# Spectral mixing after a short convolution on one core: who issues the output stores, and which buffer the half tiles use

## The chip, the core and the metric

The kernel runs on one core of one Trainium2 chip. The time is the device time of one execution in microseconds; a time given without more is the median of five runs. A profile is one more execution, recorded by the hardware profiler, and it has its own time and its own span (first to last instruction).

The engines are PE (TensorE), DVE (VectorE), ACT (ScalarE), POOL (GpSimd) and SP (SyncE). Data between memory and the core's buffers goes through 16 DMA engines. SP and POOL issue the transfers here: the profile calls SP's queue "hardware_dynamic" (q1) and POOL's "software_dynamic" (q0).

## What is computed

The input x has 8 batches of 3264 rows and 192 columns, in float32. First a causal convolution of seven taps runs down the rows, with one softmax-normalised set of taps for each of eight groups of 24 columns. Then the rows are transformed (`rfft`), the lowest 64 modes are multiplied by complex 192 x 192 matrices, one per mode, and transformed back; the result is added to its input and passed through a 192 x 192 matrix with a rectifier:

```python
X = np.fft.rfft(x, axis=1)                      # x: result of the convolution
Y[:, :64] = einsum('bmd,mde->bme', X[:, :64], w_r + 1j * w_i)
u = x + np.fft.irfft(Y, n=S, axis=1)
out = u + np.maximum(u @ w_ch, 0)               # 8 x 3264 x 192, float32
```

(The second line is shortened: the reference does it in real and imaginary parts.)

## The kernel before

**Stages.** The rows of a batch are cut into 25 full tiles of 128 rows and a half tile of 64. Batches go in four pairs (q = 0 to 3). Until about 53 us POOL issues the loads of x (L149), converted to bfloat16 on the way; PE convolves them with banded matrices held in the tile `band` (L305), and ACT and DVE copy the result into `xall`, where it stays. PE also computes the 64 modes as matmuls with cosine and sine tables. Until about 107 us the mode matrices are loaded by POOL (L426) into `arena` and `cc`, and PE applies them. `band` is read by the convolution alone. `arena` is free of the mode matrices when the last stage begins.

**The last stage, from about 108 us.** The list `duos` holds 55 items in the order in which they are worked. There are 52 items of work on tiles and three numbers among them (items 2, 8 and 11), which stand for the preparation of the next pair's coefficients. The tile items are:

- four items of two neighbouring tiles of one pair (items 0, 1, 3, 4), each stored with two transfers of 192 KB at L578;
- 45 items of one tile of two pairs, that is of four batches (items 5 to 52, but for the numbers and the half tiles), each stored with one transfer of 384 KB at L573;
- item 14, the half tiles of all eight batches (`("h",)`), stored with four transfers of 96 KB at L554, each from 64 partitions;
- the last two, items 53 and 54, of one tile of one pair, stored with one transfer of 192 KB each at L563.

For each item PE multiplies the transposed convolution result by the channel matrix (`c_part`, L494, twelve matmuls) and adds the first part of the inverse transform (`m_part(n, 0)`, L514, or L506 for the half tiles). ACT rectifies in place (`relu`, L540). PE adds the second part (`m_part(n, 1)`), and `finish` lets DVE add `xall` into an output buffer (L565; L546 for the half tiles; L560 for the single tiles) and issues the store. The order is written out by hand in the loop at the end: for each n, `m_part` and `relu` of item n, `c_part` of item n + 1, then the second `m_part` and `finish` of item n - 1. Four PSUM tiles (`za`, `zb`, two of each) take turns.

**Output buffers.** Six buffers of 3 KB per partition lie in `arena`:

```python
NO = 6
outs = [arena[:, OB * i:OB * (i + 1)]... for i in range(NO)]
...
o = outs[n % NO]
```

A buffer is written again by the item whose number is six higher (a number in the list leaves its turn out). DVE waits until the store from it has landed. The half tiles (item 14) use buffer 2, which item 20 uses next.

**Who issues.** SP issues all stores but the four of the half tiles, which POOL issues. POOL's last transfer before those is a load at L225, at 99 us. SP's only earlier transfer is the load of the taps. Each of SP's and POOL's queues works in order, and an issue waits for the DVE addition that it stores.

Of the kernel before, what the change touches and what calls it, by code (L numbers as in the profile page):

```python
# [12 lines left out]
F32 = mybir.dt.float32  # L13
# [6 lines left out]
def kernel(  # L20
# [9 lines left out]
    nc = tc.nc  # L30
# [22 lines left out]
    def sb(name, shape, dtype, **kw):  # L53
        return pool.tile([P] + shape, dtype, tag=name, name=name, **kw)
# [23 lines left out]
    band = sb("band", [H, 2 * P], BF16)  # L78
# [18 lines left out]
    NO = 6  # L97
    OB = 2 * 2 * 2 * D
    outs = [arena[:, OB * i:OB * (i + 1)].bitcast(F32).rearrange("p (k d) -> p k d", k=2) for i in range(NO)]
    assert NO * OB <= NW * WGB  # L100
    pos = [0]

    def temp(n, dtype):
# [36 lines left out]
    def slot(q, t):  # L140
        return NT * q + t
# [48 lines left out]
    for g in range(4):  # L190
        dst, srcv = band[32 * g:32 * g + 32, :, 32 * g:32 * g + PW], pk3[32 * g:32 * g + 32, :, :]
# [213 lines left out]
    for k, u in enumerate(units):  # L405
# [5 lines left out]
        if k:  # L411
            q, t0, n = units[k - 1]
# [117 lines left out]
    duos = [((q, t), (q, t + 1)) for q in range(2) for t in (0, 2)]  # L530
# [3 lines left out]
    for k, item in ((2, 1), (8, 2), (11, 3), (14, ("h",))):  # L534
        duos.insert(k, item)

    def relu(n):
        duo, zt = items[n]
        w = D * len(duo) if duo[0] != "h" else 2 * D
        nc.scalar.activation(out=zt[:, :, 0:w], in_=zt[:, :, 0:w], func=ACT.Relu)  # L540

    def finish(n):
        duo, zt = items[n]
        o = outs[n % NO]
        if duo[0] == "h":
            nc.vector.tensor_tensor(out=o[:, :, :].rearrange("p k (a d) -> p k a d", a=2),  # L546
                                    in0=zt[:, :, 0:2 * D].rearrange("p k (a d) -> p k a d", a=2),
                                    in1=xall[:, NF:NF + NT * (NQ - 1) + 1:NT, 0, :].rearrange(
                                        "p (k a) d -> p k a d", k=2), op=ALU.add)
            for k in range(2):  # L550
                for h, r in enumerate(ROWS):
                    dst = bass.AP(tensor=out.tensor, offset=out.offset + ((4 * k + (h ^ k)) * S + P * NF) * D,
                                  ap=[[D, HALF], [2 * S * D, 2], [1, D]])
                    nc.gpsimd.dma_start(out=dst, in_=o[r, k, :].rearrange("p (a d) -> p a d", a=2))  # L554
            return
        (q0, t0), (q1, t1) = duo[0], duo[-1]
        s = [slot(*u) for u in duo]
        ov = o[:, :, :].rearrange("p k (i d) -> p (k i) d", i=2)
        if len(duo) == 1:
            nc.vector.tensor_tensor(out=ov[:, 0:2, :], in0=zt[:, :, 0:D], in1=xall[:, s[0], :, :], op=ALU.add)  # L560
            dst = bass.AP(tensor=out.tensor, offset=out.offset + (2 * q0 * S + P * t0) * D,
                          ap=[[D, P], [S * D, 2], [1, D]])
            nc.sync.dma_start(out=dst, in_=ov[:, 0:2, :])  # L563
            return
        nc.vector.tensor_tensor(out=o[:, :, :].rearrange("p k (i d) -> p i k d", i=2),  # L565
                                in0=zt[:, :, 0:2 * D].rearrange("p i (k d) -> p i k d", k=2),
                                in1=xall[:, s[0]:s[1] + 1:s[1] - s[0], :, :].rearrange("p k i d -> p i k d"),
                                op=ALU.add)
        if t0 == t1:

            dst = bass.AP(tensor=out.tensor, offset=out.offset + (2 * q0 * S + P * t0) * D,
                          ap=[[D, P], [S * D, 4], [1, D]])
            nc.sync.dma_start(out=dst, in_=ov)  # L573
        else:
            for i in range(2):
                dst = bass.AP(tensor=out.tensor, offset=out.offset + ((2 * q0 + i) * S + P * t0) * D,
                              ap=[[D, P], [P * D, 2], [1, D]])
                nc.sync.dma_start(out=dst, in_=ov[:, i:4:2, :])  # L578

    N = len(duos)  # L580
# [42 lines left out]
    for n in range(N + 1):  # L623
        if is_duo(n) and duos[n] != ("h",):
            m_part(n, 0)
            relu(n)
        if n + 1 < N and n > 0:
            if is_duo(n + 1):
                c_part(n + 1)
                if duos[n + 1] == ("h",):  # L630

                    m_part(n + 1, 0)
                    relu(n + 1)
            else:
                q, zt = items[n + 1]
                for c in range(2):
                    zw_part(q, c, zt[:, c, :])
                for act, w in enumerate(QUARTERS):
                    zw_copy(zw[:, q, :, w, :], zt[:, :, 0:2 * D].rearrange("p c (b e) -> p c b e", b=4)[:, :, w, :],
                            act)  # L640
        if is_duo(n - 1):
            m_part(n - 1, 1)
            finish(n - 1)
# [30 lines left out]
```

## Time and profile before

| | |
|---|---|
| median of five runs | 179.85 us (179.24 to 180.22) |
| the profiled execution: time | 180.22 us |
| the profiled execution: span | 178.4 us |
| PE, DVE, ACT, POOL busy | 147.1, 113.4, 98.3, 68.3 us |
| granted PE clock, mean | 0.985 |
| memory read, written | 39.40 MB, 20.05 MB |
| stores issued by SP, 384 KB | 45, landing 4.6 us after the issue (median) |
| stores issued by SP, 192 KB | 10, landing after 2.9 us |
| stores issued by POOL, 96 KB | 4, landing after 3.2 us |
| POOL's queue q0 | 36224 packets, 20.08 MB |
| SP's queue q1 | 26624 packets, 19.69 MB |

Busy time is the time in which an engine executes; a DMA issue counts as busy on POOL and not on SP. "Landing" is the time from the start of the issue until the transfer's semaphore is complete, so that it holds the issue, the time in the queues, the data and the completion. A chain of waits is followed back from the last instruction; it ends with the last instruction of an engine and does not show what a store takes after that.

### The profile page before, as it was taken

The numbers are of one execution on the slowest core, as the hardware profiler recorded it, in microseconds if no ns is written. First come the engines' busy times: TensorE is split into PE (matmuls) and PEld (weight loads), VectorE is DVE, ScalarE is ACT, GpSimd is POOL, SyncE is SP. The second block draws the span as 40 slices with busy tenths as digits, with TensorE's granted clock in tenths as the row PEclk, the third lists the DMA queues.
The fourth block names the chain that finished last, engine by engine and source line by source line (L and its number), as shares of the span: only waits on it lengthen the run. The fifth ranks groups of instructions, "written<-read, shape, count | busy, mean of one in ns | idle before, by whom it ended". The sixth has DMA issues, their size and how long they took to land.

```text
span 178.4 us, 6302 instructions
## 1 busy us (share of the span) xinstructions
PE 147.1 (82%) x2736; PEld 108.4 (61%) x2736; DVE 113.4 (64%) x161; ACT 98.3 (55%) x135; POOL 68.3 (38%) x113
## 2 busy tenths in 40 slices
PE   0046789999999998797767679999999999999940
PEld 0033456666666665575555566966777888888820
DVE  1879564765866584344435262695787888888870
ACT  8165755544554636154354455767566777666630
POOL 7999979868865644424336100000140000000000
PEclk9999999999999999789999999999999999999997
DMA  3999999999999999999999970569789999999994
GB/s 43 169 176 188 190 190 189 192 192 194 188 191 192 204 206 207 206 207 207 206 206 206 206 116 4 174 220 329 256 218 365 366 336 365 362 352 353 299 371 166
DMA packets 62875, 40.17 MB, mean 225 GB/s; under 512 B 28800, under 2 KB 62784, under 8 KB 62848
## 3 DMA queue, kind: packets, MB, share of 16 engines
q0 software_dynamic: 36224, 20.08, 81.0%
q1 hardware_dynamic: 26624, 19.69, 32.9%
q8 instruction: 21, 0.34, 0.8%
q14 instruction: 6, 0.05, 0.1%
HBM read 39.40 MB, written 20.05 MB: 333 GB/s over the span
## 4 chain that ended last, share of the span: by engine, by line
DMA 45%; PE 30%; POOL 15%; issue 4%; DVE 3%; POOLq 0%; DVEq 0%
DMA arena<-in_moe_w_i_dram 18%; DMA xall<-in_x_dram 18%; POOL xall L149 10%; PE za L514 8%; PE zb L514 7%; PE za L494 7%; DMA cc<-in_moe_w_i_dram 7%; PE zb L494 5%; DMA out_dram<-arena 2%; DVE arena L565 2%; POOL arena L426 1%; POOL xall L219 1%; POOL out_dram L554 1%; PE zb L521 1%; DVE arena L560 1%
## 5 line engine op out<-in xcount | busy, mean ns | idle before, releaser
L149 POOL DMA_DIRECT2D xall<-in_x_dram x48 | 38.4, 808 | 6.9 <-DMA xall<-in_x_dram 4.5
L305 PE MATMUL z<-xall,band 64*64 64x192 bf16 (+3 forms) x816 | 27.6, 264 | 14.7 <-ACT band L193 10.7
L325 DVE CAST xall<-z 128x768 bf16<-128x768 f32 (+1 forms) x24 | 24.5, 1021 | 14.0 <-PE z L305 12.3
L305 PEld LDWEIGHTS <-band 64*64 64x64 bf16 x816 | 18.4, 110 | 23.2 <-ACT band L193 11.0
L323 ACT CAST xall<-z 128x768 bf16<-128x768 f32 (+1 forms) x24 | 20.4, 850 | 20.7 <-PE z L305 20.6
L494 PEld LDWEIGHTS <-cc 64*128 64x128 bf16 x600 | 27.2, 94 | 6.3 <-issue 1.4
L565 DVE TENSOR_TENSOR arena<-za,xall 128x768 f32<-128x768 f32 x26 | 24.6, 956 | 5.6 <-ACT zb L540 1.7
L540 ACT ACTIVATE za<-za 128x768 f32<-128x768 f32 (+1 forms) x27 | 21.0, 783 | 8.8 <-PE za L514 8.6
L565 DVE TENSOR_TENSOR arena<-zb,xall 128x768 f32<-128x768 f32 x23 | 21.9, 957 | 4.7 <-ACT za L540 1.8
L540 ACT ACTIVATE zb<-zb 128x768 f32<-128x768 f32 (+1 forms) x25 | 19.6, 782 | 9.0 <-PE zb L514 8.7
L331 PE MATMUL low<-xall,ftab 128*128 128x384 bf16 x100 | 22.0, 348 | 0.0
L385 PEld LDWEIGHTS <-xall 128*128 128x128 bf16 x300 | 18.5, 104 | 3.2 <-issue 0.3
L360 DVE COPY cc<-r 128x1024 bf16<-128x1024 bf16 (+1 forms) x16 | 10.2, 671 | 13.4 <-ACT xs L450 6.2
L514 PE MATMUL za<-mixa,ftab 64*128 64x384 bf16 (+1 forms) x120 | 18.2, 304 | 0.0
L514 PE MATMUL za<-mixa,fsin 64*128 64x384 bf16 (+1 forms) x120 | 18.1, 304 | 0.0
L494 PE MATMUL za<-wc,cc 64*128 64x192 bf16 x318 | 18.0, 243 | 0.1
L514 PE MATMUL zb<-mixa,ftab 64*128 64x384 bf16 (+1 forms) x100 | 16.1, 313 | 0.4 <-ACT zb L540 0.4
L514 PE MATMUL zb<-mixa,fsin 64*128 64x384 bf16 (+1 forms) x100 | 16.1, 313 | 0.0
L494 PE MATMUL zb<-wc,cc 64*128 64x192 bf16 x282 | 15.9, 243 | 0.0
L514 PEld LDWEIGHTS <-ftab 64*128 64x128 bf16 x220 | 11.9, 94 | 4.2 <-issue 2.0
L358 ACT COPY cc<-r 128x1024 bf16<-128x1024 bf16 (+1 forms) x9 | 8.9, 990 | 10.2 <-PE r L385 8.0
L554 POOL DMA_DIRECT2D out_dram<-arena x4 | 2.4, 617 | 29.5 <-DVE arena L546 29.5
(109 smaller groups left out, 184.0 us busy)
## 6 DMA issues: line engine op xcount, KB each, us to landing
out_dram<-arena SPq DMA_DIRECT2D x45, 384.0 KB, 4.6
xall<-in_x_dram POOLq DMA_DIRECT2D x24, 192.0 KB, 7.5
xall<-in_x_dram POOLq DMA_DIRECT2D x16, 240.0 KB, 7.1
arena<-in_moe_w_r_dram POOLq DMA_DIRECT2D x12, 288.0 KB, 9.2
arena<-in_moe_w_i_dram POOLq DMA_DIRECT2D x12, 288.0 KB, 10.2
out_dram<-arena SPq DMA_DIRECT2D x10, 192.0 KB, 2.9
xall<-in_x_dram POOLq DMA_DIRECT2D x8, 144.0 KB, 6.7
cc<-in_moe_w_r_dram POOLq DMA_DIRECT2D x4, 288.0 KB, 11.7
```

The costliest lines, as they stand in the source:

```text
L149: nc.gpsimd.dma_start(out=xall[:, s0:s0 + nf, i, :], in_=src)
L305: mm = nc.tensor.matmul(ov[c], band[r, h, c.start + shift + 64 * (r is UP and c is LO): c.start + shift + 64 * (r is UP and c is LO) + 64] ...
L323: nc.scalar.copy(out=dst, in_=srcv)
L325: nc.vector.tensor_copy(out=dst, in_=srcv)
L331: nc.tensor.matmul(xp, ftab[:, t, :], xall[:, slot(q, t), :, :], start=(t == 0), stop=False, skip_group_check=True)
L358: nc.scalar.copy(out=out, in_=in_)
L360: nc.vector.tensor_copy(out=out, in_=in_)
L385: nc.tensor.transpose(tp[:, P * k:P * k + P], src, ident[:])
L494: nc.tensor.matmul(zt[:, i, D * k:D * k + D], cc[r, q, 3 * t + j, :], wc[r, j, :], start=(k == 0 and j == 0), stop=False, skip_group_check ...
L514: nc.tensor.matmul(zt[:, i, D * k:D * (k + w)], tabs[c][r, t, :], zw[r, q:q + w, c, QUARTERS[which], :], start=False, stop=end and k + w = ...
L540: nc.scalar.activation(out=zt[:, :, 0:w], in_=zt[:, :, 0:w], func=ACT.Relu)
L565: nc.vector.tensor_tensor(out=o[:, :, :].rearrange("p k (i d) -> p i k d", i=2), in0=zt[:, :, 0:2 * D].rearrange("p i (k d) -> p i k d", k=2),
```

## The change

The stores of the 45 four-batch items and of the first of the two single tiles (item 53) are issued by POOL. The four stores of the half tiles are issued by SP, and so is the last single tile, as before. The half tiles get a seventh buffer in the bytes of `band`. The other items take the six old buffers in turn, without the half tiles and the three numbers being counted: items 0, 1, 3, 4, 5, 6 have the buffers 0 to 5, item 13 has buffer 4, and item 20 has buffer 4 again.

```diff
+    outs.append(band[:, :, :].rearrange("p h c -> p (h c)")[:, 0:OB].bitcast(F32).rearrange("p (k d) -> p k d", k=2))
...
+    buffers = []
+    for duo in duos:
+        buffers.append(NO if duo == ("h",) else sum(b < NO for b in buffers if b is not None) % NO
+                       if isinstance(duo, tuple) else None)
...
-        o = outs[n % NO]
+        o = outs[buffers[n]]
...
-                    nc.gpsimd.dma_start(out=dst, in_=o[r, k, :].rearrange("p (a d) -> p a d", a=2))
+                    nc.sync.dma_start(out=dst, in_=o[r, k, :].rearrange("p (a d) -> p a d", a=2))
...
-            nc.sync.dma_start(out=dst, in_=ov[:, 0:2, :])
+            (nc.gpsimd if n < N - 1 else nc.sync).dma_start(out=dst, in_=ov[:, 0:2, :])
...
-            nc.sync.dma_start(out=dst, in_=ov)
+            nc.gpsimd.dma_start(out=dst, in_=ov)
```

## The prediction

> **What bounds the kernel now.** I read the page first, then the chain of waits near the end, the windows of the last 66 us, the waits of DVE and SP, and the rows of the store lines. From 112 us on the kernel only produces output items and stores them. The windows (stretch, its length, then busy us of PE, PEld, DVE, ACT, POOL, the granted clock, DMA share, GB/s):
>
> ```profile
> 145.00:155.00 10.00, 10.00 (x181) 8.35 (x178) 8.50 (x9) 6.99 (x9) 0.00 (x0) 1.00 1.05 351
> 155.00:165.00 10.00, 10.00 (x180) 8.35 (x178) 8.32 (x10) 6.85 (x10) 0.00 (x0) 1.00 1.05 354
> ```
>
> PE never pauses and POOL is idle. The clock is full. The start of each item's L494 group in the timeline gives the pace, and the one break in it:
>
> ```profile
> 133.33 0.66 PE L494 MATMUL zb<-wc,cc 64*128 64x192 bf16 x12
> ...
> 134.47 0.66 PE L494 MATMUL zb<-wc,cc 64*128 64x192 bf16 x12
> ...
> 134.82 1.82 DVE L565 TENSOR_TENSOR arena<-za,xall 128x768 f32<-128x768 f32 x2 [0.60 <-DMA out_dram<-arena]
> ...
> 135.84 0.67 PE L494 MATMUL za<-wc,cc 64*128 64x192 bf16 x12
> ```
>
> The pace is 1.145 us an item (134.47 - 133.33). Item 20 has to wait 0.60 us for buffer 2, which the half tiles (item 14) still hold. PE's next group should start at 135.62 and starts at 135.84, so the break costs PE 0.22 us, once. The chain of waits then ends on DVE:
>
> ```profile
> 170.84 0.42 DVE arena L565
> 171.26 0.46 issue
> 171.72 0.55 DVE arena L560
> 172.26 0.00 issue
> 172.27 0.05 DVEq L560
> 172.32 0.04 issue
> 172.36 0.56 DVE arena L560
> ```
>
> The last addition ends at 172.92 but the span at 178.44: 5.5 us are store. The store lines' own rows say why (duration ns min/median/max; landing in us after the issue):
>
> ```profile
> L573 SPq DMA_DIRECT2D out_dram<-arena x45: 372/372/1219, 118.9 to 171.8; - x45
> DMA to landing us min/median/max: 2.5/4.6/5.2
> ```
>
> ```profile
> L563 SPq DMA_DIRECT2D out_dram<-arena x2: 533/668/803, 172.3 to 172.9; - x2
> DMA to landing us min/median/max: 4.6/4.7/4.7
> ```
>
> A 384 KB store can land in 2.5 us; the usual one takes 4.6. The last single tile (192 KB) takes 4.6 too, while the first 192 KB stores at L578 landed in 2.0. So it stands 2.6 us behind earlier stores. In the trace's landing events most of the 16 DMA engines finish a store of 158 to 165 us after 2.35 to 2.5 us, but four or five finish up to 2.4 us later. An engine falls behind where an instruction fetch (16 KB, 0.94 us on one engine, at 137.7, 144.0, 151.7, 159.5 and 165.4 us) sits in it, and it regains only 0.085 us per item. That regain is the pace less the drain: 384 KB at the 371 to 373 GB/s that full slices show is 1.06 us, against 1.145. The burst of five stores after 168.8 us then adds about 1 us on all engines. The profiled execution took 180.22 us (span 178.44 and 1.78 around it), 0.37 above the median of 179.85. I take the difference from the span and carry it to the median.
>
> **The half tiles.** They leave the ring of six buffers and get a seventh (band, last read by the convolution), so item 20 waits for item 13's buffer, long landed. Gain 0.22 us, and nothing waits for the seventh buffer. Their four stores move from POOL (four issues of 0.61 us) to SP (0.37 to 0.5 us each), behind SP's last L578 store of 118.3 us. SP then has nothing but the last tile, 44 us later. Cost nothing; were SP held up, only this buffer would be late.
>
> **45 + 1 stores from SP to POOL.** SP's issue is 0.37 us for a store. On POOL the nearest row is L149 (738/772/1035 ns). The loads of it with the same 512 rows take 0.74 to 0.79, so 0.76. POOL wakes later: L546 ends at 128.42 and POOL starts at 128.71 (0.29 us), SP 0.03 us after its addition. One store thus takes at most 0.29 + 0.76 = 1.05 us of POOL, under the pace of 1.145. POOL is otherwise idle since 99.3 us, so behind each waiting store only the next one queues.
>
> From the start of a POOL issue to its first packet are 1.22 us (128.71 to 129.93), from SP's 0.91. A POOL store with empty DMA engines so lands about 0.29 + 1.22 + 0.14 (issue 0.76 for 0.62) + 0.95 to 1.06 of data + 0.37 = 3.0 us after its addition, against 2.5 now. A buffer is wanted again after 6 x 1.145 - 0.96 = 5.9 us, so 2.9 us of cover remain, and the added 0.5 is hidden. Without that cover it would cost up to 0.5 us per round of six items.
>
> **The drain.** This decides. In the trace's packet records SP's stores go in packets of 768 bytes, 36 ns each. The POOL stores of L554 go in packets of 4,608 and 1,536 bytes, six and two rows each; the shortest take 178 and 65 ns. 178 ns for 4,608 bytes on 16 engines is 414 GB/s, or 0.95 us for a 384 KB store. Most of L554's packets took longer (median 295 ns, about 230 to 250 GB/s), but there only 64 partitions are read, and 178 is seen where no second packet ran. So the bounds are 0.95 and 1.7 us per store, with SP's 1.06 between. I take 0.95, since the full-width stores read all partitions. It regains 0.19 us an item instead of 0.085, and over the 30 items after 136 us that is 5.7 us per engine, more than the largest lag seen (2.4 us).
>
> The Trainium skill (DMA: Bandwidth & Descriptors, "Issuing engines are not separate DMA queues") speaks against this: stores from any engine run on the same 16 DMA engines, and another issuer saves only sequencer time. By that rule the drain stays as it is and the sum is the 0.22 us alone. The packet sizes that the two issuers show differ sixfold, which the rule leaves out.
>
> POOL writes its descriptors while DVE adds. The four L554 issues took 602 to 638 ns beside L565 additions, the weight loads of L426 610 to 622. The same skill (SBUF - State Buffer, "The DVE blocks DMA trap") warns that POOL's descriptor writing starves under some DVE operations; by it each 0.96 us addition could hold up an issue. These rows show no such delay.
>
> **The end, worked.** Item 52's addition ends at 171.80 - 0.22 = 171.58. Its POOL store: + 0.29 + 0.76 + 0.60 to the first packet = 173.2. Data behind it on all engines: 0.95 for it, 0.47 for the first single tile on POOL, 0.53 for the last on SP (192 KB at 373 GB/s), together 175.15. Last packet to landing 0.37 now (177.16 to 177.53): 175.5. For engines still behind, 0 to 0.6, I take 0.3: 175.8. From landing to the span's end 0.91 stays. 176.7 against 178.44 is -1.7 us; with the 0.22 inside, the drain brings 1.5. Bounds: if the last store lands in the 2.0 us of an idle queue, 172.73 + 2.07 + 0.91 = 175.7, -2.7; if the drain brings half, -0.9.
>
> **Forecast:** 179.85 - 1.7 = 178.2 us, own range 177.1 to 179.2. Chance 0.62.
>
> **Rival 1: the drain is no faster** (memory or the rows limit it, not packets). For it: full slices are flat at 370 to 373 GB/s. Against: weight loads of the same POOL queue wrote 206 GB/s from twice the bytes read, so the engines move 412. Then the slow engines set the end as now and only 0.22 remains: 179.6. Chance 0.18, most of it within 0.3% (0.54 us, about what a measurement can tell from no change).
>
> **Rival 2: POOL becomes the bound, slower.** Place: POOL's queue from 118.9 us. Take the longest L149 row, 1.035 us, and the wake of 0.29 each time: 1.31 per store. After 45 of them it starts the single tile at 118.9 + 59.0 = 177.9, which lands 2.06 later (0.62 issue, 0.60, 0.47, 0.37), and the span ends at 180.9: +2.4, so 182.3 us. It decides from 1.26 us per store, where the same sum gives 178.44; the median row with the wake is at 1.06. Chance 0.12.
>
> **Rival 3: POOL's stores drain at L554's usual 230 GB/s.** 1.71 us per store instead of 1.145 is 45 x 0.565 = +25 us, 205 us. The half partitions speak against it. Chance 0.05; a remaining 0.03 for smaller losses at the end. That the change does not do what it says is out: in the built program SP keeps 13 stores and POOL has the 46.
>
> **Chances and range.** Faster: 0.62 + 0.04 of rival 1 = 0.66. Same: 0.14. Slower: 0.20. The range takes the forecast's bound below (179.85 - 2.8, rounded to 177.0) and rival 1 above with 0.7 us for small losses, 180.3; rivals 2 and 3 are left out.
>
> **What would show it.** Right: the DVE wait on a store at L565 is gone; PE's L494 starts stay 1.145 apart; POOL's stores take about 0.76 us at that pace; their packets are 4,608 bytes; the last landing comes about 3 us after the last addition, not 4.6. Wrong: packets of 768 bytes or a full-slice rate of 370 (rival 1); DVE waiting on stores with POOL busy throughout (rival 2), or with POOL idle and DMA full (rival 3).

## The result: 0.4% slower, and the profile after

The change takes 180.33 us (median of 26 runs, 179.76 to 181.65). The kernel before took 179.75 us on the same chips (47 runs, 178.63 to 181.50). The ratio is 1.004, with a 95% interval of 1.0026 to 1.0054. The forecast was 178.2 us with a range of 177.0 to 180.3: wrong in direction, and just outside the range.

The two profiled executions alone would mislead. Before's took 180.22 us, above its median, and after's 179.89 us, below its own. Much of what differs from one execution to the next lies before the first output addition, which came between 111.0 and 112.3 us in eighteen profiles (in both profiles of a kernel 0.3 to 0.4 us apart, where the rest differs by 0.2). So I compare stretches counted from that addition. They leave out whatever POOL's stores may change ahead of it: on average it came 0.25 us later in the eleven profiles with them, less than the profiles scatter.

First the head of the page after, with the DMA queues (packets, MB, share of 16 engines), the costliest store group and the row of its issues:

```profile
span 178.1 us, 6295 instructions
...
PE 149.0 (84%) x2736; PEld 109.9 (62%) x2736; DVE 113.1 (64%) x161; ACT 98.3 (55%) x135; POOL 100.4 (56%) x155
...
q0 software_dynamic: 41136, 37.59, 106.1%
q1 hardware_dynamic: 3168, 2.19, 4.0%
...
L580 POOL DMA_DIRECT2D out_dram<-arena x45 | 33.9, 754 | 39.6 <-DVE arena L572 38.6
...
out_dram<-arena POOLq DMA_DIRECT2D x45, 384.0 KB, 4.4
```

17.5 MB have moved from q1 to q0; q0 has 4,912 packets more and q1 23,456 fewer. The lines have moved by seven: L573, L563 and L565 of before are L580, L570 and L572 here. The store lines' own rows, first those of the 45 stores, then those of the two single tiles:

```profile
L580 POOL DMA_DIRECT2D out_dram<-arena x45: 752/752/805, 118.1 to 171.8; - x45
...
DMA to landing us min/median/max: 3.3/4.4/5.4
```

```profile
L570 POOL DMA_DIRECT2D out_dram<-arena x1: 707/707/707, 172.5 to 172.5; - x1
L570 SPq DMA_DIRECT2D out_dram<-arena x1: 389/389/389, 172.6 to 172.6; - x1
...
DMA to landing us min/median/max: 4.1/4.2/4.3
```

The fastest store takes 3.3 us where SP's took 2.5, and the last ones 4.1 to 4.3 where SP's took 4.6 to 4.7: the tail did get shorter, by 0.4 us from the issue and not by 1.5. Whether POOL's stores did that, the experiments must say. The windows that bounded the kernel, in the same columns as before:

```profile
145.00:155.00 10.00, 10.00 (x179) 8.20 (x175) 8.32 (x10) 7.06 (x9) 6.53 (x9) 1.00 0.95 361
155.00:165.00 10.00, 10.00 (x181) 8.30 (x178) 8.50 (x9) 6.99 (x9) 6.14 (x9) 1.00 0.89 347
```

PE is as full as before and POOL, 6.1 to 6.5 of 10 us busy, has room. The chain that ends last has gone from DVE to POOL:

```profile
170.84 0.75 POOL out_dram L580
171.59 0.19 issue
171.78 0.02 POOLq L570
171.79 0.75 POOL out_dram L580
172.54 0.70 POOLq L676
```

Its last line is the end of the program on POOL (L676, which was L669), and the view stops where it starts. That line turned out to matter: it holds, on POOL, an instruction named DRAIN of 5.05 us.

### The profile page after: what moved, and what is told of

The parts are those of the page before. It is cut to its first block, busy times and chain, and to the rows that moved or that the text cites. A ratio compares the mean times of both kernels' runs of the same rounds, so it can differ in the third digit from the quotient of the medians.

```text
span 178.1 us, 6295 instructions
## 1 busy us (share of the span) xinstructions
PE 149.0 (84%) x2736; PEld 109.9 (62%) x2736; DVE 113.1 (64%) x161; ACT 98.3 (55%) x135; POOL 100.4 (56%) x155
## 4 chain that ended last, share of the span: by engine, by line
DMA 28%; PE 26%; POOL 24%; issue 13%; DVE 3%; ACT 2%; POOLq 1%; DVEq 0%; ACTq 0%
DMA arena<-in_moe_w_i_dram 18%; POOL out_dram L580 17%; PE z L307 9%; DMA cc<-in_moe_w_i_dram 6%; PE low L333 6%; POOL xall L151 4%; DMA xall<-in_x_dram 4%; PE low L387 2%; PE za L516 2%; PE za L496 2%; POOL arena L428 1%; ACT xall L325 1%; PE zb L516 1%; PE zb L496 1%; PE zb L523 1%
## 5 line engine op out<-in xcount | busy, mean ns | idle before, releaser
L580 POOL DMA_DIRECT2D out_dram<-arena x45 | 33.9, 754 | 39.6 <-DVE arena L572 38.6
L307 PE MATMUL z<-xall,band 64*64 64x192 bf16 (+3 forms) x816 | 28.4, 268 | 14.5 <-ACT band L195 10.6
L307 PEld LDWEIGHTS <-band 64*64 64x64 bf16 x816 | 18.9, 112 | 23.3 <-ACT band L195 10.9
L572 DVE TENSOR_TENSOR arena<-za,xall 128x768 f32<-128x768 f32 x26 | 24.7, 956 | 5.3 <-ACT zb L547 2.0
L572 DVE TENSOR_TENSOR arena<-zb,xall 128x768 f32<-128x768 f32 x23 | 21.9, 956 | 5.0 <-ACT zb L547 1.7
L333 PE MATMUL low<-xall,ftab 128*128 128x384 bf16 x100 | 22.7, 356 | 0.0
L387 PEld LDWEIGHTS <-xall 128*128 128x128 bf16 x300 | 19.1, 106 | 3.4 <-issue 0.7
L428 POOL DMA_DIRECT2D arena<-in_moe_w_r_dram x12 | 7.4, 614 | 16.4 <-PE low L439 11.9
```

The costliest lines, as they stand in the source:

```text
L307: mm = nc.tensor.matmul(ov[c], band[r, h, c.start + shift + 64 * (r is UP and c is LO): c.start + shift + 64 * (r is UP and c is LO) + 64] ...
L333: nc.tensor.matmul(xp, ftab[:, t, :], xall[:, slot(q, t), :, :], start=(t == 0), stop=False, skip_group_check=True)
L387: nc.tensor.transpose(tp[:, P * k:P * k + P], src, ident[:])
L580: nc.gpsimd.dma_start(out=dst, in_=ov)
```

## The experiments

Three numbers describe each profile, all from the instructions and landings in the trace: **add**, from the start of the first output addition to the end of the last; **land**, from there to the last landing of a store; **end**, from there to the end of the span. Their sum is free of the noise ahead of the first addition. Ratios are against the kernel before on the same chip, with a 95% interval.

| kernel | POOL's stores of 46 | add | land | end | sum | ratio |
|---|---|---|---|---|---|---|
| before | none | 61.05 | 4.61 | 0.91 | 66.57 | |
| before_r2 | none | 60.88 | 4.53 | 0.92 | 66.33 | |
| h_only | none | 60.80 | 4.26 | 1.17 | 66.23 | 0.998 (0.997 to 1.000) |
| h_buffer_only | none | 60.81 | 4.60 | 0.90 | 66.32 | 0.998 (0.997 to 1.000) |
| h_yet | none | 60.80 | 4.29 | 1.16 | 66.25 | 1.002 (0.999 to 1.005) |
| sp_single_own | none | 60.80 | 4.32 | 1.15 | 66.27 | 1.002 (1.000 to 1.004) |
| ring7_sp | none | 60.81 | 4.32 | 1.17 | 66.30 | 1.002 (1.000 to 1.005) |
| after | 46 | 61.00 | 4.29 | 1.22 | 66.51 | 1.004 (1.003 to 1.005) |
| after_r2 | 46 | 60.95 | 4.33 | 1.46 | 66.74 | |
| pool_only | 46 | 61.19 | 4.27 | 1.27 | 66.73 | 1.002 (1.000 to 1.005) |
| after_single_own | 46 | 60.81 | 4.48 | 1.43 | 66.72 | 1.006 (1.003 to 1.008) |
| pool_ring7 | 46 | 60.80 | 4.94 | 1.49 | 67.23 | 1.007 (1.005 to 1.009) |
| pool_then_sp | below item 44 | 61.30 | 4.61 | 0.90 | 66.81 | 1.003 (1.000 to 1.005) |
| pool_until_48 | below item 48 | 61.28 | 4.56 | 1.15 | 66.99 | 1.004 (1.001 to 1.006) |
| pool_until_30 | below item 30 | 60.81 | 4.55 | 1.60 | 66.96 | 1.004 (1.001 to 1.006) |
| ring7_until_48 | below item 48 | 60.81 | 4.92 | 1.15 | 66.88 | 1.004 (1.001 to 1.007) |
| sp_then_pool | from item 44 | 60.80 | 4.05 | 2.67 | 67.52 | 1.007 (1.004 to 1.011) |
| one_late_pool | one, the 46th | 60.87 | 4.57 | 2.30 | 67.74 | 1.007 (1.004 to 1.009) |

Without POOL's stores the sum is 66.2 to 66.6 us. With them it is 66.5 to 67.7, and the means of the two groups (66.3 and 67.0) differ by 0.7 us; without sp_then_pool and one_late_pool, which were built to end with POOL's stores, by 0.5. In the ratios no kernel with POOL's stores is below 1.002, but three of the five without them stand at 1.002 too, so a single ratio settles little.

### The two parts by themselves

h_only and h_buffer_only keep the half tiles' part alone, with their four stores on SP and on POOL. pool_only keeps the stores' part alone, on the old ring of six:

```diff
 h_only, from the change
-            (nc.gpsimd if n < N - 1 else nc.sync).dma_start(out=dst, in_=ov[:, 0:2, :])
+            nc.sync.dma_start(out=dst, in_=ov[:, 0:2, :])
...
-            nc.gpsimd.dma_start(out=dst, in_=ov)
+            nc.sync.dma_start(out=dst, in_=ov)
 h_buffer_only, from h_only
-                    nc.sync.dma_start(out=dst, in_=o[r, k, :].rearrange("p (a d) -> p a d", a=2))
+                    nc.gpsimd.dma_start(out=dst, in_=o[r, k, :].rearrange("p (a d) -> p a d", a=2))
 pool_only, from before
-            nc.sync.dma_start(out=dst, in_=ov[:, 0:2, :])
+            (nc.gpsimd if n < N - 1 else nc.sync).dma_start(out=dst, in_=ov[:, 0:2, :])
...
-            nc.sync.dma_start(out=dst, in_=ov)
+            nc.gpsimd.dma_start(out=dst, in_=ov)
```

> The half-tile part alone: seventh buffer, their four stores on SP, every other store on SP as before. If POOL's stores are what costs (theory: they end the run no earlier and add to it), this is before less the 0.22 us stall: 0.1 to 0.4 us faster than before. If moving the half tiles is what costs (rival: SP needs 3.0 us for the four issues and DVE starts the item after them 0.36 us late), the DVE start after the half tiles is late here too, by about 0.36 us, and the time is 0 to 0.5 us above before.

> Seventh buffer alone: the half tiles still issued by POOL, all else by SP. Both theories expect the 0.60 us wait of DVE to be gone and 0.22 us to be gained on PE's pace. The rival expects no late DVE start here, so this is faster than the kernel with the half tiles on SP by about 0.2 us; the theory expects the two to be equal.

> The issuers alone: 45 four-batch stores and the first single tile from POOL, half tiles on POOL in the old ring of six. Theory (POOL's stores cost at the end): slower than before by 0.5 to 1.0 us, since it has the change's loss without its 0.22. Rival (the half tiles cost): equal to before or up to 0.5 us faster. The half tiles' four issues and a four-batch store now wait for each other in POOL's queue, 4 x 0.61 + 0.75 us, so the DVE wait for buffer 2 should grow from 0.60 to 1.0 to 1.5 us.

Measured: 179.71, 179.74 and 180.5 us, beside 179.93 for before on that chip. So the loss seems to come with the stores and not with the half tiles, though pool_only's own interval reaches down to 1.000. In pool_only the wait of item 20 is gone too, against what I expected of it. The two kernels with the half tiles' part alone look 0.2% faster here, but three later ones with a seventh buffer and no POOL stores, on other chips, came out at 1.002, so that part is worth nothing that these runs can tell.

The profile says why it is worth so little. This is DVE's timeline of the change around item 14 (start, duration, what ended the idle time before):

```profile
127.20 0.96 DVE L553 TENSOR_TENSOR band<-zb,xall 128x768 f32<-128x768 f32 x1 [0.43 <-PE zb L508]
128.80 0.96 DVE L572 TENSOR_TENSOR arena<-zb,xall 128x768 f32<-128x768 f32 x1 [0.64 <-PE za L516]
```

The addition after the half tiles' starts 1.60 us after theirs. In before the same two starts were 127.46 and 128.69, 1.23 us apart. PE loses 0.18 us by that, against the 0.22 us won at item 20. The late addition reads `zb`, and the matmuls on `zb` were done at 128.33, 0.47 us before it starts. The profile puts the end of its wait down to the next matmuls, on `za`, which it does not read (done at 128.65); in before it started without them. Whether the built program makes it wait for them, the trace does not say.

To see whether it is the bytes of `band` that make the addition late, h_yet puts the seventh buffer elsewhere:

```diff
-    outs.append(band[:, :, :].rearrange("p h c -> p (h c)")...
+    outs.append(yet[:, :, :, :, :].rearrange("p t b c m -> p (t b c m)")...
```

> All stores from SP, half tiles in a seventh buffer, but in the bytes of yet instead of band. In all five kernels with band as the seventh buffer the addition after the half tiles starts 0.36 us late and PE loses 0.18 us. If that comes from band, it is gone here, and the kernel is 0.3 to 0.6 us faster than before; if it comes from the order of the buffers or of the instructions, it stays, and the time is that of the kernel with band, 0.1 to 0.4 us faster than before.

It is 0.36 us late there as well, and in every kernel with a seventh buffer. So it isn't the place. What it is stays open.

### A repeat of both kernels

before_r2 and after_r2 are the two kernels once more, for a second profile of each.

> The kernel before once more, for a second profile of its end. Both theories: the last addition waits for its buffer (0.51 us in the first profile), the last landing comes 4.3 to 4.7 us after it.

> The change once more, for a second profile. Its first profile had a span 0.4 us under the median of its runs. If the end varies, the wait of the last addition for its buffer is 0.8 us here, as in the other two kernels with POOL's stores, and the last addition 0.3 us later; if the stretch before the stores varies, the first addition comes 0.3 to 0.6 us later and the end is as in the first profile.

One time each: 179.64 and 180.53 us. In after_r2 the first addition came 0.42 us later than in after and the last one waited no longer: most of the difference between the two lies before the stores, and 0.24 us in end. Add is the same within 0.1 us for both pairs. Land is 0.2 to 0.3 us shorter with the change, and end 0.3 to 0.55 us longer.

### Is a POOL store faster to drain?

light_sp and light_pool thin the work of PE, ACT and DVE so that the stores alone set the pace: of `c_part` one matmul group of three is left, and ACT and DVE work on half the columns of the four-batch items. The two differ in who issues the stores.

```diff
-            for j in range(3) if k in ks else ():
+            for j in range(1) if k in ks else ():
...
-        nc.scalar.activation(out=zt[:, :, 0:w], in_=zt[:, :, 0:w], func=ACT.Relu)
+        nc.scalar.activation(out=zt[:, :, 0:w // 2], in_=zt[:, :, 0:w // 2], func=ACT.Relu)
...
+        e = HD if t0 == t1 else D
```

(the addition of a four-batch item then covers columns 0 to e)

> All stores from SP, and the work ahead of them thinned so that the stores are the bound: a third of the channel product is computed, and ACT and DVE work on half of the columns of the four-batch items. Stores per us in full stretches measure the drain by itself. Both theories: 1.05 to 1.07 us per 384 KB store, 368 to 373 GB/s.

> The same thinned work (a third of the channel product, half of the columns on ACT and DVE), four-batch stores from POOL. The prediction's term: 0.95 us per 384 KB store, 414 GB/s, because of the large packets. The rival, which the end of the change's profile speaks for (366 GB/s while full): 1.03 to 1.07 us, as from SP, so that larger packets win nothing once all 16 engines are full. If POOL's issue were the bound it would be 0.75 to 0.8 us.

The window from 135 to 165 us of light_sp, then of light_pool:

```profile
DMA packets 14774, 11.07 MB, mean 369 GB/s; under 512 B 444, under 2 KB 14769, under 8 KB 14769
```

```profile
DMA packets 3183, 11.22 MB, mean 374 GB/s; under 512 B 455, under 2 KB 908, under 8 KB 3178
```

The times are 174.61 and 176.21 us; light_pool's first addition came 2.3 us later, so the rates are what to compare. The packets are a fifth in number, but the rate is 369 against 374 GB/s. Where POOL's stores follow each other without a gap, one takes 0.991 us (397 GB/s), against SP's 1.055. POOL also pauses now and then, which takes most of that back. So full engines do move POOL's stores faster, in 6% less time, where the forecast had 10%: its 0.95 us was the shortest packet's time on all engines, and full engines never showed it. And in the change they were not kept full. This is the stretch from 172.5 to 175.5 us, behind the last addition, with the busy share of the DMA engines in 40 slices (tenths):

```profile
DMA  3959499999994994879695994969976998999998
...
DMA packets 466, 1.10 MB, mean 366 GB/s; under 512 B 53, under 2 KB 272, under 8 KB 466
```

Several slices are half empty, though the engines are busy for 97% of the stretch in all, so that this is only a part of the difference from 397. In before, from 171 to 175 us, every slice is full, at 371 GB/s:

```profile
DMA  9999999999999999999999999999999999999999
```

So at the end of this kernel the larger packets bring no more bandwidth.

### Which end of the store stream costs it

pool_then_sp gives SP the stores from item 44 on, and sp_then_pool gives POOL only those:

```diff
 pool_then_sp, from the change (single tiles: both on SP)
-            nc.gpsimd.dma_start(out=dst, in_=ov)
+            (nc.gpsimd if n < 44 else nc.sync).dma_start(out=dst, in_=ov)
 sp_then_pool, from the change
-            nc.gpsimd.dma_start(out=dst, in_=ov)
+            (nc.sync if n < 44 else nc.gpsimd).dma_start(out=dst, in_=ov)
```

> The change, with the last nine four-batch stores and both single tiles on SP. Theory: what costs is the end (the wake and issue of POOL for the last stores, the last SP store sharing the DMA engines with POOL's large packets, 0.27 us more from the last landing to the end of the span). With SP at the end those go, the engines that lag are caught up by then, and it is faster than before by 0.3 to 1.0 us. If instead the drain of POOL's stores leaves a backlog all along, or the half tiles cost, it is as slow as the change: 0.3 to 0.7 us above before.

> The change turned round: the four-batch stores up to item 43 from SP, the last nine and the first single tile from POOL, half tiles as in the change. If POOL's later start (wake 0.29, issue 0.75) costs at the end, where the DMA engines stay full until the last landing, this is as slow as the change: 0.4 to 0.8 us above the kernel that moves the half tiles alone, 0.2 to 0.6 us above before. If POOL costs in the run up to item 43 (its pauses, the ring that is nearly used up), this is as fast as the half tiles alone: 0.1 to 0.4 us faster than before.

pool_then_sp refutes what I expected of it: with the last stores on SP its end is as short as before's (0.90 us), but its add is the longest, 61.30 us, and it takes 180.26 us against 179.93. The cost is not at the end alone.

sp_then_pool has the earliest last landing of all (4.05 us after the last addition) and is among the slowest (181.29 us against 179.88): 2.67 us lie between the last landing and the end of the span. The rows of the program's last line say where. These are the DRAINs of POOL and SP (ns min/median/max, first and last start) in before, in the change and in sp_then_pool:

```profile
L669 POOLq DRAIN  x3: 46/93/6279, 130.1 to 178.2; - x3
L669 SPq DRAIN  x3: 7/7/7, 177.6 to 177.9; - x3
```

```profile
L676 POOLq DRAIN  x3: 46/106/5050, 172.3 to 177.8; - x3
L676 SPq DRAIN  x3: 7/7/7, 177.1 to 177.6; - x3
```

```profile
L676 POOLq DRAIN  x3: 46/93/6085, 171.9 to 178.5; - x3
L676 SPq DRAIN  x3: 7/7/7, 176.5 to 178.3; - x3
```

The DRAIN that follows POOL's last store takes 5 to 7 us; it ends 0.5 to 1.9 us after that store has landed, in every profile with output stores from POOL. In sp_then_pool that ends at 171.91 + 6.09 = 177.99 us, 1.9 us after the last landing (176.10), while SP has been through with its own waits since 176.47. In these profiles the span ends 0.82 to 0.85 us after SP is through (0.96 once), or 0.78 us after POOL's DRAIN ends, whichever comes later. Before had such a DRAIN too, after the four half-tile stores; it was over 42 us before the end.

one_late_pool tests this by itself: every store on SP but one, the first single tile's.

```diff
 one_late_pool, from h_only
-            nc.sync.dma_start(out=dst, in_=ov[:, 0:2, :])
+            (nc.gpsimd if n < N - 1 else nc.sync).dma_start(out=dst, in_=ov[:, 0:2, :])
```

> Seventh buffer and half tiles by SyncE as in the change; of all other stores only the first single tile's, the last but one of the kernel, is issued by POOL. Theory DRAIN (the end of the program waits for POOL's DRAIN, which ended 4.8 to 5.8 us after the issue of POOL's last store, later than the last landing): a store issued at about 172.2 us by POOL lets the DRAIN end at 177.0 to 178.0 us; from the last landing to the end of the span 1.2 to 2.7 us where the same kernel with SyncE's stores alone had 1.17, and a ratio of 1.000 to 1.005 where that had 0.998. Theory BUFFERS (POOL's stores land later, so buffers come free later): one store that nobody waits for changes nothing, ratio 0.998.

```profile
L676 POOLq DRAIN  x3: 46/93/6348, 172.4 to 179.3; - x3
L676 SPq DRAIN  x3: 7/7/7, 177.4 to 179.0; - x3
```

One store of 192 KB costs 1.1 us behind the last landing: end is 2.30 us against 1.17 of h_only. Land is 0.3 us longer too, and the time is 180.98 us against 179.72 for before. Its DRAIN ends at 178.77, 1.5 us after the last landing, and the other engines, which wait for one another there, wait for it. BUFFERS, which forecast 0.998, is out for this store. So it is shown that a late DRAIN of POOL's holds up the end of the program. In the change itself its part is small: the DRAIN ends at 172.28 + 5.05 = 177.33 and the span at 178.12. SP was through at 177.10, so without POOL the end would have come at 177.92: the DRAIN costs 0.19 us there, and 0.24 us in after_r2 by the same sum.

### What is left when the DRAIN is out of the way

pool_until_48 and pool_until_30 stop POOL's stores early enough for the DRAIN to be over:

```diff
 from the change (single tiles: both on SP); 30 in the second kernel
-            nc.gpsimd.dma_start(out=dst, in_=ov)
+            (nc.gpsimd if n < 48 else nc.sync).dma_start(out=dst, in_=ov)
```

> The change, with the stores of the last five four-batch items (from item 48 on) and of the first single tile issued by SyncE; POOL has its last store near 166.5 us. Theory DRAIN: its DRAIN is over by 172 us, before the last landing, so from the last landing to the end 0.9 to 1.17 us, 0.2 to 0.5 us less than the change; ratio 1.001 to 1.002. Theory BUFFERS: the stores of 40 items still land later and the last items still wait, VectorE's additions take 61.0 to 61.3 us; ratio 1.002 to 1.004. Both may hold a part.

> The change, with the stores of four-batch items from item 30 on and of the first single tile issued by SyncE: POOL issues about 22 of 45, the last near 144 us. Theory DRAIN: nothing of it reaches the end, ratio as with SyncE's stores alone, 0.998 to 0.999. Theory BUFFERS: only where POOL's stores are still in use do buffers come late, and PE catches no delay up, so what VectorE lost by item 30 stays: 0.1 to 0.2 us, ratio 0.999 to 1.000. A cost of POOL's stores that is there before any of them is awaited (in the stretch before the first addition) would leave 1.002.

180.63 and 180.65 us, against 179.72: still 0.35% slower than before. So the late DRAIN isn't all. pool_until_48 came out as BUFFERS forecast (add 61.28 us), pool_until_30 as neither theory did (add 60.81 us). In pool_until_48 DVE waits for stores again (its waits from 112 us on, total, times, longest):

```profile
DVE arena L567 <- DMA out_dram<-arena: 0.3, 1, 0.3
DVE arena L572 <- DMA out_dram<-arena: 0.3, 1, 0.3
```

From 158 to 165 us a store of POOL's is done on half of the DMA engines 3.1 to 3.2 us after its issue, SP's in before after 2.4 to 2.5. A buffer is free only when the slowest engine is done: 4.9 to 5.4 us after the addition here, 4.4 to 4.8 in before, 4.4 to 5.0 in the change. pool_until_30 has no such wait. Its end is long, 1.60 us, because SP is held up by 0.46 us between its last wait and its DRAIN, with nothing in the trace to show for it.

pool_ring7 gives POOL's stores more time: after the half tiles all items go round seven buffers.

```diff
-        buffers.append(NO if duo == ("h",) else sum(b < NO for b in buffers if b is not None) % NO
-                       if isinstance(duo, tuple) else None)
+        buffers.append(None)
+    order = [k for k, duo in enumerate(duos) if isinstance(duo, tuple)]
+    at = order.index(14)
+    for k, n in enumerate(order):
+        buffers[n] = k % NO if k < at else NO if k == at else (5, 0, 1, 2, 3, 4, NO)[(k - at - 1) % (NO + 1)]
```

> The change, but after the half tiles all items go round seven buffers, the seventh among them, where the change goes round six and leaves the seventh unused: every store has an item of 1.19 us more to land. Theory BUFFERS: no addition waits for a store any more, so VectorE's additions from first to last take 60.6 to 60.8 us where the change took 61.0; 0.2 to 0.5 us less than the change, ratio 1.001 to 1.003. Theory DRAIN: the end is set by POOL's last store plus 4.8 to 5.8 us; an earlier last addition moves that store too, but DMA engines that are full to the end take as long as before: ratio 1.003 to 1.005.

Add falls to 60.80 us as BUFFERS said, and the time does not fall: 181.1 us against 179.72. Land grows to 4.94 us. The ratio, 1.007, is above what either theory forecast. What DVE no longer waits for seems to stand in the DMA engines instead. The two kernels that give the single tiles buffers of their own, in the two halves of the seventh, had said the same:

```diff
+            ov = outs[NO][:, n - (N - 2), :].rearrange("p (i d) -> p i d", i=2)
```

(after_single_own adds this to the change, sp_single_own to h_only)

> The change, with the two single tiles in the two halves of the seventh buffer, so that their additions wait for no store of the ring. Theory (the ring is short at the end: the last addition waits until the store of item 48 has landed, and POOL makes that later): the last addition starts 0.2 to 0.5 us earlier and the time falls by 0 to 0.4 us against the change, to 0 to 0.4 us above before. Rival (the DMA engines are full to the end anyway): the last addition starts earlier, but the last landing does not, and the time is that of the change, 0.3 to 0.7 us above before.

> All stores from SP, half tiles in the seventh buffer, and the two single tiles in its two halves. It joins the parts that won or may win: 0.2 to 0.6 us faster than before by the theory of the short ring, 0.1 to 0.3 us faster (the half tiles' part alone) if the full DMA engines set the end.

The last addition of after_single_own ends 0.18 us earlier relative to the first, and the last store lands 0.19 us later after it: 180.74 us against 179.77. sp_single_own took 180.13 us, where I had expected less than before.

The last pair takes both suspects away. ring7_until_48 has the ring of seven and POOL's stores below item 48 only; ring7_sp is the same with SP's alone.

```diff
 from pool_ring7 (single tiles: both on SP); in ring7_sp all on nc.sync
-            nc.gpsimd.dma_start(out=dst, in_=ov)
+            (nc.gpsimd if n < 48 else nc.sync).dma_start(out=dst, in_=ov)
```

> Ring of seven buffers after the half tiles, half tiles by SyncE; POOL issues the stores of the 41 four-batch items below item 48, SyncE the last five of four batches and both single tiles. POOL's DRAIN is over near 172 us and no addition waits for a store. If DRAIN and BUFFERS are all that POOL's stores cost, nothing is left: VectorE's additions 60.8 us, from the last landing to the end 0.9 to 1.2 us, ratio within 0.002 of the same kernel with SyncE's stores alone (ring7_sp). If POOL's stores cost something else as well (as the 1.0037 of the kernel with 22 of them in the middle may say), the two differ by 0.4 to 0.8 us and the ratio stays at 1.003 to 1.005.

> The same kernel as ring7_until_48 with every store issued by SyncE: the control for it on the same chip. Both theories: VectorE's additions 60.8 us, 1.15 us from the last landing to the end, ratio 0.998 to 1.001.

180.47 and 180.18 us; the ratios 1.004 and 1.002 have overlapping intervals and are within the 0.002 that I had named for "nothing is left". The times alone show no further cost. In the profiles add and end are equal (60.81; 1.15 and 1.17), and land is 4.92 against 4.32 us. The stretch from 135 to 165 us in ring7_until_48, then in ring7_sp, where both make an item every 1.145 us:

```profile
DMA packets 2974, 10.51 MB, mean 350 GB/s; under 512 B 419, under 2 KB 845, under 8 KB 2968
```

```profile
DMA packets 14448, 10.83 MB, mean 361 GB/s; under 512 B 443, under 2 KB 14442, under 8 KB 14442
```

With POOL 0.32 MB less has gone out, which is 0.87 us at the 370 GB/s of full engines; 54 us after the first addition it is 0.30 MB less, so it is not that the window falls differently. The last store is done on half the engines 4.13 us after the last addition instead of 3.09, and on the last engine 0.60 us later. The first of these has a nearer cause than the engines: SP issued its last stores late. These are its two single tiles, in ring7_until_48 and in ring7_sp:

```profile
172.97 1.79 SPq L573 DMA_DIRECT2D out_dram<-arena  x2
```

```profile
171.41 1.33 SPq L573 DMA_DIRECT2D out_dram<-arena  x2
```

SP's last four issues took 0.80 to 1.01 us each, in ring7_sp 0.37 to 0.71, so the last store left SP 1.30 us after its addition instead of 0.18. From its issue it is done on half the engines in 2.8 us, in ring7_sp in 2.9. Why the issues take longer is not in the trace. For the last engine, a reading that fits but is not shown is that POOL's stores reach the engines later, so that these have holes, and that what they miss is still to be moved when the additions are over. Pauses that would make such holes can be seen in POOL's timeline of the change, around 164 us:

```profile
163.07 0.75 POOL L580 DMA_DIRECT2D out_dram<-arena  x1 [0.39 <-DVE arena L572]
164.88 2.38 POOL L580 DMA_DIRECT2D out_dram<-arena  x3 [1.06 <-DVE arena L572]
```

The store due at 164.21 goes out at 164.88, 0.67 us late. The store due at 136.74 is 1.06 us late, 24 stores earlier. The additions that they wait for were in time; the trace shows no cause.

## Why the prediction was wrong, step by step

**The half tiles: mechanism right, gain given back.** The wait for their buffer is gone and PE wins the 0.22 us at item 20, but the addition behind the half tiles starts 0.36 us late and takes 0.18 of it.

**POOL's cost per store: right.** 0.752 us for an issue (0.76 forecast; at most 0.805 us, beside DVE's additions) and 0.30 us from the addition's end to its start (0.29). POOL keeps the pace but for the two pauses. (One row was misread: the issues of L426 took 610 to 655 ns, not up to 622. That changes nothing.) Rival 2 did not happen: the single tile's store left POOL at 172.5 us, not at 177.9.

**The buffer cover: nearly used up, not 2.9 us.** The sum took a store on empty DMA engines, 3.0 us after its addition. Measured from the addition, POOL's 384 KB stores landed after 4.8 us in the median and 5.7 at the longest, so that 1.1 and 0.2 us of the 5.9 were left. In the steady stretch that was just enough: one wait of 0.3 us in after_r2, none in after. The last items are less than an item apart, and a single tile's addition is shorter. There the last addition, which in h_only follows the one before it by 0.47 us, waits for item 48's store: it starts 0.17 and 0.15 us later than that with the change, 0.18 and 0.00 in the two profiles of before, 0.5 in pool_only and pool_then_sp.

**The drain: this step failed, and with it 1.5 of the 1.7 us.** I took 0.95 us for a 384 KB store from the shortest packets. Full engines took 0.99 at best (SP's 1.055), and at the end, where they were not all full, 366 GB/s, no better than SP's 371. By 0.99 us the lagging engine regains 0.155 us an item instead of 0.19, and that did happen: at the end the slowest engine is 0.3 to 0.6 us behind the middle one, where in before it was 1.1 to 1.4. But the middle itself came later. In before most engines were through with a store 2.35 to 2.5 us after its issue, that is, nearly idle between stores. There nothing covers POOL's later start of 0.6 us. I had counted that latency against the buffers and not against the engines. And the end was worked as if the engines were empty when item 52's store reached them, though it comes in the burst of stores after 168.8 us, which I had put at 1 us myself: the sum has that store done 2.97 us after its addition, measured were 3.9 us on half of the engines and 4.5 on the last. So land fell from 4.57 us (mean of two profiles) to 4.31, 0.26 us and not 1.5. And it does not take POOL's stores to get there: h_only, with every store on SP, has 4.26, and three more such kernels 4.29 to 4.32. Against h_only POOL's stores brought nothing. The rule of the Trainium skill that spoke against the change (DMA: Bandwidth & Descriptors, "Issuing engines are not separate DMA queues") was the better guide here: by it the drain does not change with the issuer, and at the end of the two kernels the runs give 371 and 366 GB/s. With engines kept full they do show a difference, 373 and 397 GB/s.

**"From landing to the span's end 0.91 stays": wrong by 0.3 to 0.55 us.** Two things are in it. POOL's DRAIN ends later than SP's waits (0.19 and 0.24 us). And SP goes through its waits for the stores' semaphores one by one, 0.06 us each, in the order of the semaphores: in before the last store to land is the last of them, in the change others follow (SP is through 0.08 us after the last landing in before, 0.20 and 0.39 in the change). This second part is not POOL's doing: in h_only SP is through 0.32 us after the last landing, and end is 1.17 us. The row for the first was in the profile of before: a DRAIN of 6.28 us on POOL after stores of 96 KB. I had not opened the program's last line, because nothing waited for it then.

**The sum.** Forecast -1.7. In the two pairs of profiles add changed by 0.0, land by -0.26 and end by +0.43: +0.17 us. The medians differ by +0.58. The rest, some 0.4 us, cannot be put in a place from two profiles of a kernel. Against h_only, which has the same buffers and no store from POOL, the change's two profiles are longer by 0.17 us in add, 0.05 in land and 0.17 in end: 0.4 us, where the ratios 1.004 and 0.998 differ by 1.0 us. Over all profiles, the means of the eleven with POOL's stores stand above those of the seven without by 0.1 us in add, 0.1 in land and 0.45 in end; without sp_then_pool and one_late_pool end differs by 0.25. **Rival 1** (drain no faster, 179.6 us) came nearest, since against h_only the drain brought nothing; it lacked the costs in add and end, so its time was low as well. **Rival 3** (230 GB/s) is out.

**What stays open:** why an addition is 0.36 us late as soon as there is a seventh buffer, why POOL pauses, why SP's last issues take longer in ring7_until_48, whether POOL's pauses and later starts are what lengthens land there, and where more than half of the change's 0.58 us lies. No version that was run is clearly faster than the kernel before.

## What to carry to other kernels

Before moving stores to another engine, look at what that engine does at the end of the program: POOL's DRAIN lasted 5 to 7 us here and ended 0.5 to 1.9 us after POOL's last store had landed, so POOL's last one should be well ahead of the end. The time of a single packet is no bandwidth until full engines have shown it. Work the end of a kernel with the backlog that the engines have by then, not from empty engines; and a later start of a transfer is hidden only while the engines have a backlog, which is to be read engine by engine and not from the slowest one. Where the noise ahead of a change is as large as its effect, compare from the first instruction behind that noise. And compare each part of a change with a kernel that has the rest of it: against before, the shorter land looked like the work of POOL's stores, but h_only has it too.

## What the runs showed of the hardware

- POOL's DRAIN after its last output store took 5.05 to 6.77 us (the change and h_buffer_only) and ended 0.46 to 1.89 us after that store had landed (pool_until_48 and sp_then_pool).
- POOL's stores go in packets of 4,608 bytes (178 ns each, median) and SP's in 768 (36 ns). Over 30 us of light_pool and light_sp the rates are 374 and 369 GB/s; where stores follow each other without a gap, 397 and 373.
- A POOL store of 384 KB is done on half of the engines 2.7 us after the start of its issue at the earliest, 3.0 after its addition (the change); SP's after 2.4 of either (before).
- POOL put off a store by 1.06 us and, 24 stores later, by 0.67 us, at the same places in the change and in ring7_until_48, with nothing in the trace that it waits for.
